# The last quarter of a maxout FFN by Strassen's seven products on row halves of TensorE

## The chip, the core and the metric

The kernel runs on one NeuronCore of one Trainium2 chip. The metric is the device time of one execution in microseconds (us). The kernel before takes 2413.1 us, the median of three runs (2412.13 to 2416.76). The profiled execution spans 2409.3 us from its first to its last instruction.

Engines are written as in the profile: PE is TensorE's matmul, PEld its weight load, DVE VectorE, ACT ScalarE, POOL GpSimd, and SPq, ACTq and POOLq are the queues that issue transfers.

## The reference

All in fp32: a long convolution along the sequence by means of a Fourier transform, and behind it a feed-forward layer that takes the maximum of three products.

```python
# x, v: (4, 12544, 128); pos_emb: (12544, 64)
h_filt = (np.maximum(pos_emb @ w1, 0.0) @ w2) * np.exp(-0.01 * pos)[:, None]
u = x * v
y = irfft(rfft(u, 2 * S) * rfft(h_filt, 2 * S), 2 * S)[:, :S, :]
t = (x * y).reshape(4 * 12544, 128)
# moe_w1..3: (128, 768), moe_w_out: (768, 128)
h = np.maximum(np.maximum(t @ moe_w1, t @ moe_w2), t @ moe_w3)
out = h @ moe_w_out
```

The kernel subtracts `moe_w1` once from the other two, so that each hidden block needs two products (the "up" products): max(a, b, c) = a + max(0, b - a, c - a). The part `a @ w_out` is linear in the token and is one product with a folded matrix, `lin` = moe_w1 @ moe_w_out.

## The kernel before

There are four batches. Each has 32 tiles of 392 tokens (4 x 98), laid out with the 128 model dimensions on the partitions. While the FFN of batch b runs, the convolution of batch b + 1 runs beside it in slots between its products. Beside the last batch nothing runs.

A matmul is always given as two halves of 64 output columns each, which go to the two column halves of the array:

```python
def halves_mm(out, lhsT, rhs, start, stop):
    for h in range(2):
        nc.tensor.matmul(out[64 * h:64 * h + 64], lhsT[:, 64 * h:64 * h + 64], rhs,
                         start=start, stop=stop, skip_group_check=True)      # L132
```

A tile goes through four helpers. `t_load` fetches the tile's part of the convolution's last stage (`zt`) and of x (`xT`). `t_last` makes the token tile `gt`. `up` makes one of six hidden blocks of 128 x 392. `down` adds that block's product with `w_out` to one bank of PSUM and stores the tile after the sixth.

```python
def t_last(i):
    ...
    for s in range(4):
        for a in range(2):
            halves_mm(y[:, s, a * h:a * h + h], zt[:, a, s * D:(s + 1) * D],
                      f4p[:, a, :], s == 0 and a == 0, True)                  # yps
    ... # gt = yps * xT, on DVE (L535)

def up(i, f):
    rhs = gs[i][:].rearrange("d p n -> d (p n)")
    h = hp.tile([P, N], FP32, tag="hid", name="hid")
    pa = hps.tile([P, 512], FP32, tag="hps", name="pa")
    halves_mm(pa[:, 0:N], w_sb[1][:, f * P:(f + 1) * P], rhs, True, True)
    nc.scalar.activation(h[:], pa[:, 0:N], Relu)                              # L545
    pb = hps.tile([P, 512], FP32, tag="hps", name="pb")
    halves_mm(pb[:, 0:N], w_sb[2][:, f * P:(f + 1) * P], rhs, True, True)
    nc.vector.tensor_tensor(out=h[:], in0=h[:], in1=pb[:, 0:N], op=ALU.max)   # L548
    return h

def down(i, f, h):
    if f == 0:
        pos_[i] = ops.tile([D, 512], FP32, tag="ops", name="ops")
        halves_mm(pos_[i][:, 0:N], lin[:], gs[i][:]..., True, False)
    halves_mm(pos_[i][:, 0:N], wo_sb[:, f, :], h[:], False, f == NF - 1)
    if f < NF - 1:
        return
    ...
    nc.scalar.copy(o[:]..., pos_.pop(i)[:, 0:N])                              # L561
    nc.scalar.dma_start(dst, o[:])

for n, (b, i) in enumerate(tiles):          # 4 batches x 32 tiles
    ...
    for f in range(NF):                     # 6 hidden blocks
        ...
        h = up((b, i), f)
        if late is not None:
            down(*late)                     # the block before
        late = ((b, i), f, h)
        if f == 3 and n + 1 < len(tiles):
            t_last(tiles[n + 1])
        ...
```

In the prologue, the filter's little network (`pm`, products on row halves of the array) starts with one group, then a transpose and a product for the window (`window_back`), then the other groups:

```python
warm_up(30)
...
for i in range(9):
    if i < 8:
        mlp_in(i)
    if i == 0:
        window_back()
    if i:
        mlp_out(i - 1)
```

Of the kernel before, what the change touches and what calls it, by code (L numbers as in the profile page):

```python
# [9 lines left out]
FP32 = mybir.dt.float32  # L10
I32 = mybir.dt.int32
U16 = mybir.dt.uint16
ALU = mybir.AluOpType
ACTF = mybir.ActivationFunctionType
PSUM = bass.MemoryType.PSUM
P = 128
# [8 lines left out]
N1 = 90  # L25
# [45 lines left out]
def kernel(  # L71
# [15 lines left out]
    nc = tc.nc  # L87
    NG, _, _, B, NB = x.shape
    FO, S = posT.shape
    D = w2.shape[1]  # L90
# [21 lines left out]
    back_d = nc.inline_tensor(np.eye(P, dtype=np.float32)[:, order].copy(), name="back_const").ap()  # L112
    eye_d = nc.inline_tensor(np.eye(P, dtype=np.float32), name="eye_const").ap()

    w_sb = [const.tile([D, DFF], FP32, name=f"w_sb{i}") for i in range(3)]
    wo_sb = const.tile([P, NF, D], FP32, name="wo_sb")
    lin = const.tile([D, D], FP32, name="lin")
    eye = const.tile([P, P], FP32, name="eye")
    f1 = const.tile([NB, 2 * N1], FP32, name="f1")
    f4 = const.tile([N1, 2, NB], FP32, name="f4")  # L120
    spec = const.tile([P, N1, 2, D], FP32, name="spec")
# [102 lines left out]
    utp = ctx.enter_context(tc.tile_pool(name="utp", bufs=2))  # L224
    pro = ExitStack()
    pin = pro.enter_context(tc.tile_pool(name="pin", bufs=1))
    lwp = pro.enter_context(tc.tile_pool(name="lwp", bufs=3))
    fin = ExitStack()
    inp0 = fin.enter_context(tc.tile_pool(name="inp0", bufs=3))
# [46 lines left out]
    def warm_up(n):  # L276

        ps = fps.tile([P, 1024], FP32, tag="cv", name="pw", bufs=2)
        for _ in range(n):
            halves_mm(ps[:, 0:256], warm[:, 0:P], warm[:], True, True)  # L280

    def window_back():
        pw = fps.tile([P, 1024], FP32, tag="cv", name="pw", bufs=2)
        nc.tensor.transpose(pw[:, 0:64 + HH], win[:], eye[0:64 + HH, 0:64 + HH])
        nc.scalar.copy(winT[:], pw[:, 0:64 + HH])
        nc.tensor.matmul(pw[0:64 + HH, 512:512 + P], winT[:],
                         back[:].rearrange("p r t -> p (r t)"), start=True, stop=True)
        nc.scalar.copy(winr[:].rearrange("n r t -> n (r t)"), pw[0:64 + HH, 512:512 + P])
# [164 lines left out]
    def conv_steps(b, done):  # L453


        out = []

        def at(slot, late, fn, *args):
            out.append((slot, late, len(out), fn, args))

        per_pair = 170 / (NK + 0.6 * (NU - done))
        for u in range(done, NU):
            s = (u - done) * 0.6 * per_pair + 9
            at(max(0, int(s) - 10), 0, u_load, b, u)
            at(int(s) - 6, 0, u_mul, u)
            at(int(s) - 5, 0, u_planes, u)
            at(int(s) - 4, 0, u_dma, u)
            at(int(s), 0, u_join, u)  # L470
            for h in range(2):
                at(int(s + 1 + 0.3 * per_pair * h), 1, u_first, u, h)
        s0 = int((NU - done) * 0.6 * per_pair) + 10
        for g in range(NK):
            s = s0 + int(g * per_pair)
            at(s - 5, 0, w_load, g, 0)
            at(s - 3, 0, h_load, g)
            at(s, 1, g_second, g)
            at(s + 1, 0, w_load, g, 1)
            at(s + 1, 0, g_butterfly, g)  # L480
            at(s + 2, 0, g_swap, g)
            at(s + 3, 0, g_re, g)
            at(s + 4, 0, g_im, g, True)
            at(s + 6, 0, g_unfold, g)
            at(s + 7, 1, g_third, b, g)
        slots = {}
        for s, _, _, fn, args in sorted(out, key=lambda r: r[:3]):
            slots.setdefault(s, []).append((fn, args))
        return slots
# [23 lines left out]
    def t_last(i):  # L513
        zt = zts.pop(i)
        ps = cps.tile([P, 512], FP32, tag="cv", name="yps")
        g = hp.tile([D, 4, NB], FP32, tag="g", name="gt", bufs=2)
        y = ps[:, 0:N].rearrange("d (p n) -> d p n", p=4)
        if i[0] == 0:
            for s in range(4):
                for c in range(2):  # L520
                    halves_mm(y[:, s, :], zt[:, c, s * D:(s + 1) * D], f4[:, c, :],
                              s == 0 and c == 0, c == 1)
        else:

            h = NB // 2
# [3 lines that stand above are left out]
                              f4p[:, a, :], s == 0 and a == 0, True)  # L529
            y = y.rearrange("d p (a m) -> d p m a", a=2)  # L530
        xT = xTs.pop(i)
        if i[0] == 0:
            nc.vector.tensor_tensor(out=g[:], in0=y, in1=xT[:], op=ALU.mult)  # L533
        else:
            nc.vector.tensor_tensor(out=g[:].rearrange("d p (m a) -> d p m a", a=2), in0=y,  # L535
                                    in1=xT[:].rearrange("d p (m a) -> d p m a", a=2),
                                    op=ALU.mult)
        gs[i] = g

    def up(i, f):  # L540
        rhs = gs[i][:].rearrange("d p n -> d (p n)")
        h = hp.tile([P, N], FP32, tag="hid", name="hid")
        pa = hps.tile([P, 512], FP32, tag="hps", name="pa")
        halves_mm(pa[:, 0:N], w_sb[1][:, f * P:(f + 1) * P], rhs, True, True)
        nc.scalar.activation(h[:], pa[:, 0:N], Relu)  # L545
        pb = hps.tile([P, 512], FP32, tag="hps", name="pb")
        halves_mm(pb[:, 0:N], w_sb[2][:, f * P:(f + 1) * P], rhs, True, True)
        nc.vector.tensor_tensor(out=h[:], in0=h[:], in1=pb[:, 0:N], op=ALU.max)  # L548
        return h
# [4 lines that stand above are left out]
            halves_mm(pos_[i][:, 0:N], lin[:], gs[i][:].rearrange("d p n -> d (p n)"), True,  # L554
                      False)
# [3 lines that stand above are left out]
        gs.pop(i)  # L559
        o = op_.tile([D, 4, NB], FP32, tag="o", name="ot")  # L560
        nc.scalar.copy(o[:].rearrange("d p n -> d (p n)"), pos_.pop(i)[:, 0:N])  # L561
        dst = outT.rearrange("d (p b n) -> d p b n", b=B, n=NB)[:, 4 * i[1]:4 * i[1] + 4, i[0], :]
        nc.scalar.dma_start(dst, o[:])

    def run(steps):
        for fn, args in steps:
# [31 lines left out]
        ps = fps.tile([P, 1024], FP32, tag="cv", name="ps1")  # L598
        first_halves(ps, lhs, table, dst, nc.scalar.copy)

    warm_up(30)
    raws.append(load_raw(*jobs[0], nc.sync))
    u_load(0, 0)
    u_load(0, 1)
# [3 lines left out]
    for i in range(9):  # L608
        if i < 8:
            mlp_in(i)  # L610
        if i == 0:
            window_back()
        if i:
            mlp_out(i - 1)
    signs()
# [132 lines left out]


    hp = ctx.enter_context(tc.tile_pool(name="hp", bufs=3))  # L750
    f4p = hp.tile([N1, 2, NB // 2], FP32, name="f4p", bufs=1)
    nc.scalar.dma_start(f4p[:], f4p_d)
    inq = ctx.enter_context(tc.tile_pool(name="inq", bufs=2))
    planes = [hp.tile([P, 2, 4, P], U16, name=f"planes{i}", bufs=1) for i in range(3)]
    for t in planes:
        nc.gpsimd.memset(t[:].rearrange("p h s n -> p (h s n)"), 0)
    op_ = ctx.enter_context(tc.tile_pool(name="op", bufs=2))
    wp = ctx.enter_context(tc.tile_pool(name="wp", bufs=3))
    hh = ctx.enter_context(tc.tile_pool(name="hh", bufs=3))
    cvp = ctx.enter_context(tc.tile_pool(name="cvp", bufs=3))  # L760
    cps = ctx.enter_context(tc.tile_pool(name="cps", bufs=4, space=PSUM))
    hps = ctx.enter_context(tc.tile_pool(name="hps", bufs=3, space=PSUM))
    ops = ctx.enter_context(tc.tile_pool(name="ops", bufs=1, space=PSUM))
    state = {"turn": cps, "pair": (wp, hh), "cv": (cvp, cps), "xb": 3}


    tiles = [(b, i) for b in range(B) for i in range(NT)]
    late = None
    for n, (b, i) in enumerate(tiles):
        if i == 0:  # L770
            beside = {}
            if b + 1 < B:
                beside = conv_steps(b + 1, EARLY if b == 0 else 0)
        if n == 0:
            t_load(*tiles[0])
            t_load(*tiles[1])
            t_last(tiles[0])
        for f in range(NF):

            if i < NT - 2:  # L780
                if f == 0:
                    t_load(*tiles[n + 2])
            elif i == NT - 1 and f < 2 and n + 1 + f < len(tiles):
                t_load(*tiles[n + 1 + f])
            h = up((b, i), f)
            if late is not None:
                down(*late)
            late = ((b, i), f, h)
            if f == 3 and n + 1 < len(tiles):
                t_last(tiles[n + 1])  # L790
            s = i * NF + f
            run(beside.pop(s, ()))
            if s == NT * NF - 1:
                assert not beside, sorted(beside)
    down(*late)


# [35 lines left out]
```

## Time and profile before

| engine | busy us | share of 2409.3 us |
|---|---|---|
| PE | 2393.4 | 99% |
| PEld | 1463.2 | 61% |
| DVE | 1286.4 | 53% |
| ACT | 1026.7 | 43% |
| POOL | 314.2 | 13% |

The chain of waits that ended last is 97% PE. The granted clock of TensorE is 1.0 throughout.

Three habits help with this profile. A program's matmul appears as two records and two weight loads, since fp32 takes two passes; a `halves_mm` is thus four records. A record's duration holds its way through the array too, so the rate is read from the distance of starts. And a row of groups gives busy us, mean ns of one, then the idle time of that engine ahead of the group and what ended it; for an engine that is not the bound, such idle time costs nothing.

### The profile page before, as it was taken

The page shows a single profiled execution, that of the slowest core. Times are in us where ns is not written, and L with a number is a line of the kernel's source. Part 1 is how long each engine was busy: PE and PEld are TensorE (multiplying, and loading weights), DVE is VectorE, ACT ScalarE, POOL GpSimd, SP SyncE. Part 2 cuts the span into 40 slices and gives each one's busy share as a digit, 9 for nine tenths or more (in the row PEclk, how much of TensorE's full clock was granted, in tenths as well). Part 3 has the DMA queues.
Part 4 walks back from the last instruction along what each step waited for, and adds up shares of the span by engine and source line. Part 5 has one row for each costly group of instructions (what it writes and reads, how often), then busy time and mean ns, then how long its engine had stood idle before and what let it go on. Part 6 is the DMA issues. An engine that isn't in the chain of part 4 may idle for free.

```text
span 2409.3 us, 63290 instructions
## 1 busy us (share of the span) xinstructions
PE 2393.4 (99%) x26089; PEld 1463.2 (61%) x26089; DVE 1286.4 (53%) x2719; ACT 1026.7 (43%) x1981; POOL 314.2 (13%) x349
## 2 busy tenths in 40 slices
PE   9999999999999999999999999999999999999999
PEld 8988866655555556666656546666665654444444
DVE  5588834466666645446666644446666642222222
ACT  2688834444444434444444424444444432222222
POOL 2022211011111101101111111101111100000000
PEclk9999999999999999999999999999999999999999
DMA  7778879767767659967777859968777742222221
GB/s 171 179 240 266 278 167 179 162 190 196 214 194 211 175 125 187 182 174 207 219 207 215 219 124 182 189 162 213 214 215 209 215 113 61 55 62 53 64 53 36
DMA packets 544553, 408.21 MB, mean 169 GB/s; under 512 B 390244, under 2 KB 436381, under 8 KB 544265
## 3 DMA queue, kind: packets, MB, share of 16 engines
q1 hardware_dynamic: 421760, 315.25, 53.8%
q10 hardware_dynamic: 117129, 74.31, 10.7%
q0 software_dynamic: 5376, 14.62, 2.1%
q8 instruction: 205, 3.36, 0.6%
q14 instruction: 83, 0.68, 0.1%
HBM read 295.76 MB, written 84.67 MB: 158 GB/s over the span
## 4 chain that ended last, share of the span: by engine, by line
PE 97%; DMA 1%; ACT 1%; DVE 0%; issue 0%; SPq 0%; ACTq 0%; POOL 0%; DVEq 0%
PE ops L132 24%; PE pb L132 21%; PE pa L132 21%; PE ps L132 13%; PE ps L141 7%; PE yps L132 5%; PE sps L688 3%; PE pm L303 1%; PE gps L674 1%; PE pst L341 1%; PE pw L132 1%; DMA hd<-ht 1%; ACT ht L693 0%; DMA xT<-in_x_dram 0%; DVE xt L424 0%
## 5 line engine op out<-in xcount | busy, mean ns | idle before, releaser
L548 DVE TENSOR_TENSOR hid<-hid,pb 128x392 f32<-128x392 f32 x768 | 431.8, 562 | 789.4 <-PE pb L132 510.2
L545 ACT ACTIVATE hid<-pa 128x392 f32<-128x392 f32 x768 | 381.9, 498 | 799.3 <-PE pa L132 630.1
L132 PE MATMUL pa<-gt,w_sb 128*64 128x392 f32 x3072 | 640.7, 493 | 1.1 <-DVE gt L533 1.1
L132 PE MATMUL pb<-gt,w_sb 128*64 128x392 f32 x3072 | 639.6, 492 | 1.4 <-ACT hid L545 1.2
L132 PE MATMUL ops<-hid,wo_sb 128*64 128x392 f32 x3072 | 639.5, 492 | 0.1
L132 PEld LDWEIGHTS pb<-gt,w_sb 128*64 128x64 f32 x3072 | 225.8, 137 | 283.0 <-issue 257.1
L132 PEld LDWEIGHTS ops<-hid,wo_sb 128*64 128x64 f32 x3072 | 227.1, 137 | 278.9 <-issue 228.8
L424 POOL TENSOR_TENSOR xt<-xt,xs 128x512 f32<-128x512 f32 x135 | 172.5, 1278 | 969.6 <-DVE xs L423 778.7
L132 PEld LDWEIGHTS pa<-gt,w_sb 128*64 128x64 f32 x3072 | 201.8, 137 | 111.3 <-issue 67.4
L141 PEld LDWEIGHTS ps<-f,uT 98*64 98x64 f32 x4096 | 178.0, 137 | 47.4 <-issue 44.7
L132 PEld LDWEIGHTS ps<-ab,wt 128*64 128x64 f32 x2880 | 168.4, 137 | 52.4 <-issue 26.8
L132 PE MATMUL ps<-ab,wt 128*64 128x128 f32 x2880 | 190.9, 274 | 1.8 <-DVE ab L431 1.7
L132 PEld LDWEIGHTS ps<-spec,wt 128*64 128x64 f32 x2880 | 168.0, 137 | 37.8 <-issue 34.2
L132 PE MATMUL ps<-spec,wt 128*64 128x128 f32 x2880 | 189.5, 273 | 1.4 <-issue 1.4
L141 PE MATMUL ps<-f,uT 98*64 98x90 f32 x4096 | 188.0, 241 | 0.0
L449 DVE TENSOR_TENSOR zs<-ps,z 128x256 f32<-128x256 f32 x270 | 102.0, 419 | 96.6 <-ACT z L447 94.3
L413 ACT ACTIVATE xs<-xt 64x512 f32<-64x512 f32 x180 | 113.1, 628 | 71.1 <-DVE xt L158 58.9
L431 DVE TENSOR_TENSOR ab<-xt 128x256 f32<-128x256 f32 x360 | 136.0, 419 | 1.6
L419 DVE TENSOR_TENSOR xt<-xt,ht 128x512 f32<-128x512 f32 x180 | 124.2, 690 | 15.6 <-ACT ht L693 15.2
L356 POOL COPY planes<-ut 128x784 uint16<-128x784 uint16 x90 | 76.2, 847 | 426.5 <-DVE ut L336 301.1
L145 ACT COPY spec<-ps 128x360 f32<-128x360 f32 (+1 forms) x132 | 71.8, 546 | 137.0 <-PE ps L141 136.8
L132 PEld LDWEIGHTS yps<-f4p,zt 90*64 90x64 f32 x3072 | 107.3, 138 | 34.4 <-issue 32.3
(86 smaller groups left out, 1824.4 us busy)
## 6 DMA issues: line engine op xcount, KB each, us to landing
wt<-wt_const SPq DMA_DIRECT2D x360, 256.0 KB, 4.8
ht<-hd SPq DMA_DIRECT2D x270, 256.0 KB, 4.5
zd<-zs ACTq DMA_DIRECT2D x180, 256.0 KB, 4.6
zt<-zd SPq DMA_DIRECT2D x192, 180.0 KB, 3.8
ut<-in_xr_dram SPq DMA_DIRECT2D x128, 196.0 KB, 3.6
ut<-in_vr_dram SPq DMA_DIRECT2D x128, 196.0 KB, 4.3
xT<-in_x_dram SPq DMA_DIRECT2D x512, 49.0 KB, 3.0
out_dram<-ot ACTq DMA_DIRECT2D x128, 196.0 KB, 4.0
```

Of the source, the lines that this page charges most:

```text
L132: nc.tensor.matmul(out[64 * h:64 * h + 64], lhsT[:, 64 * h:64 * h + 64], rhs, start=start, stop=stop, skip_group_check=True)
L141: nc.tensor.matmul(ps[64 * c:64 * c + 64, 256 * i + r * N1:256 * i + (r + 1) * N1], a[:, r, :], table[:, c * N1:(c + 1) * N1], start=(i % ...
L145: copy(dst, ps[:].rearrange("p (s m) -> p s m", m=256)[:, :, 0:2 * N1].rearrange("p s (r k) -> p k r s", r=2))
L356: nc.gpsimd.tensor_copy(pl_[:, :, :, 0:NB], a[:].bitcast(U16).rearrange("p s (n h) -> p h s n", h=2))
L413: nc.scalar.mul(xs[0:64], xt[64:128], -1.0)
L419: nc.vector.tensor_tensor(out=xt[:], in0=xt[:], in1=hts[g][:, 0], op=ALU.mult)
L424: (nc.gpsimd if apart else nc.vector).tensor_tensor(out=xt[:], in0=xt[:], in1=xs[:], op=ALU.add)
L431: nc.vector.tensor_tensor(out=ab[:, :, q, :], in0=y[:, :, 0, :], in1=y[:, :, 1, :], op=op)
L449: nc.vector.tensor_tensor(out=zs[:, a], in0=ps[:, 0:256], in1=z1[:], op=op)
L545: nc.scalar.activation(h[:], pa[:, 0:N], Relu)
L548: nc.vector.tensor_tensor(out=h[:], in0=h[:], in1=pb[:, 0:N], op=ALU.max)
L688: nc.tensor.matmul(ps[64 * h:64 * h + 64, (2 * c + k) * 2 * D:(2 * c + k + 1) * 2 * D], G[:, k, c], w2x[:].rearrange("p s d -> p (s d)"), ...
```

## The change

The last batch is handled by pairs of tiles from here on, and two kinds of product are done by Strassen's method (in Winograd's form): a product of 2 x 2 blocks with seven products of blocks and not eight, for extra sums.

- Products with `w_out`: the blocks are tile 1 or 2 of the pair, lower or upper three hidden blocks, lower or upper 64 output columns. A product of blocks has 128 rows of the array, 64 columns, and the 392 tokens are cut into two halves of 196 that go to the two column halves.
- Up products: the blocks are tile 1 or 2, lower or upper 64 model dimensions, lower or upper three hidden blocks. A product of blocks has only 64 rows, so two different ones are issued together, one on the lower, one on the upper rows of the array, into different banks of PSUM. This is done for both up weights, for all pairs but the first, whose hidden blocks are made as before.
- Sums of weights (`tw`, `T`) are made once on DVE and ACT. Sums of tokens (`a_sums`) and of hidden blocks (`s1` to `s4`) are made per pair, mostly on GpSimd. Sums of products are made on DVE out of PSUM.
- The buffers of the convolution are given up before the last batch; `spec`, which held the spectrum, gives space for hidden blocks.
- In the prologue, `window_back` is called within the warm-up.

The purpose is fewer microseconds of TensorE in the stage in which the other engines have room. The core of the diff (cuts marked with ...):

```diff
-    warm_up(30)
+    warm_up(22)
+    window_back()
+    warm_up(3)
...
-        if i == 0:
-            window_back()
...
+    def products(b, i, h, X, Y):
...
+        def mm(ps, w, rhs, start):
+            for c in range(2):
+                nc.tensor.matmul(ps[64 * c:64 * c + 64, 0:H2], w, rhs[:, H2 * c:H2 * c + H2],
+                                 start=start, stop=True, skip_group_check=True)
...
+        plan = (
+            (X, "h11", wo_sb[:, 0:NC, 0:64], True, None, [(copied, "p1", X)], None),
+            (Y, "s2", tw[:, 0], True, None, [(added, "u2", "p1", Y)], None),
+            (X, "h12", wo_sb[:, NC:, 0:64], False, (m1, first), [(copied, "c11", X)], None),
+            (Y, "s3", tw[:, 1], False, (m2, second_), [(added, "u3", "p1", Y)], None),
+            (X, "s1", wo_sb[:, 0:NC, 64:128], True, None, [(added, "c22", "u3", X)], None),
+            (Y, "h22", tw[:, 2], True, (linx[:], second_), [(added, "c21", "u3", Y)],
+             (stored, 0)),
+            (X, "s4", wo_sb[:, NC:, 64:128], False, (m2, first), [(added, "c12", "u2", X)],
+             (stored, 1)),
+        )
...
-    for n, (b, i) in enumerate(tiles):
+    for n, (b, i) in enumerate(tiles[:LAST]):
...
+    conv.close()
...
+    def cycle(i, j, h):            # one of three column blocks of a pair of tiles
...
+        def mm(ps, w, at, rhs, rows, start=False):
+            for c in range(2):
+                nc.tensor.matmul(ps[64 * c:64 * c + 64, 0:N],
+                                 w[rows, at + 64 * c:at + 64 * c + 64], rhs[rows],
+                                 start=start, stop=True, skip_group_check=True)
+        def P1(v): mm(Ys[v], w_sb[1 + v], j * P, g1, LO, True)
+        def P2(v): mm(X_, w_sb[1 + v], j * P, g1, HI, True)
+        def P3(v): mm(Zs[v], w_sb[1 + v], HF_ + j * P, r1, HI)
+        def P4(v): mm(Ys[v], T[v][:, 0], j * P, g2, HI)
+        def P5(v): mm(Zs[v], T[v][:, 0], j * P, r1, LO, True)
+        def P6(v): mm(Ys[v], T[v][:, 1], j * P, r2, HI if v else LO)
+        def P7(v): mm(Ys[v], T[v][:, 2], j * P, r3, LO)
...
+        def hidden(name, a, ps, b=None, at=None):
+            at = at or ps
+            tt(out=at[:, 0:N], in0=new[b], in1=ps[:, 0:N], op=ALU.add)
+            h[name, j] = spare(name)
+            nc.vector.scalar_tensor_tensor(
+                out=h[name, j], in0=new[a], scalar=0.0, in1=at[:, 0:N], op0=ALU.max, op1=ALU.max)
...
+        return {                   # step: [products, what reads them]
+            0: [lambda: P1(a), lambda: copied("p0", Ys[a])],
+            1: [lambda: (P1(b), P2(a)),
+                lambda: (copied("p1", Ys[b]), added("t11", "p0", X_))],
+            2: [lambda: P6(a), lambda: copied("u0", Ys[a])],
+            3: [lambda: P6(b), lambda: copied("u1", Ys[b])],
+            4: [lambda: (P7(a), P2(b)),
+                lambda: (copied("v0", Ys[a]), hidden("h11", "t11", X_, "p1"))],
+            5: [lambda: P7(b), lambda: copied("v1", Ys[b])],
+            6: [lambda: (P5(a), P4(a)), lambda: (h21a(), added("t22", "v0", Zs[a]))],
+            7: [lambda: P4(b), lambda: (h21b(), sums(h, j, 0))],
+            9: [lambda: P3(a), lambda: added("t12", "u0", Zs[a])],
+            10: [lambda: P5(b), lambda: (rest22(), sums(h, j, 1))],
+            12: [lambda: P3(b), lambda: (hidden("h12", "t12", Zs[b], "u1"), sums(h, j, 2))],
+        }
...
+    for i in range(2, NT, 2):
+        h = {}
+        X, Y = banks if i % 4 == 0 else banks[::-1]
+        for j in range(NC):
+            now = cycle(i, j, h)
+            for q in range(7):
...
+                both = [now[q]] + ([before_[q + 7]] if q + 7 in before_ else [])
+                for m in range(2):
+                    for e_ in both[::-1] if m and q in (2, 5) else both:
+                        e_[m]()
+                if (j, q) == (0, 4):
+                    queue += queue_next
+                    queue_next = products(b, i, h, X, Y)
+                some_of(2 if q == 0 or (j, q) == (1, 6) else 1)
...              # loads and t_last of the next pair, its sums of tokens
+            before_ = now
```

Steps 7 to 12 of a column block are issued together with steps 0 to 5 of the next (`before_[q + 7]`), so that each step has one product on the lower and one on the upper rows. `some_of(1)` issues the next product with `w_out` of the pair before; a pair has 25 of these for its 21 steps (21 block products and 4 linear terms).

## The prediction

> **What bounds the kernel now.** I read three things in turn: the page's engine shares, the chain of waits (97% PE), and then only the stage that the change rewrites, the last of the four batches.
>
> ```profile
> PE 2393.4 (99%) x26089; PEld 1463.2 (61%) x26089; DVE 1286.4 (53%) x2719; ACT 1026.7 (43%) x1981; POOL 314.2 (13%) x349
> ```
>
> TensorE is never idle, so only fewer TensorE microseconds can help. The copies of finished output tiles date the stage (timeline of ScalarE):
>
> ```profile
> 1977.32 0.49 ACT L561 COPY ot<-ops 128x392 f32<-128x392 f32 x1 [0.82 <-PE ops L132]
> ...
> 2405.55 0.49 ACT L561 COPY ot<-ops 128x392 f32<-128x392 f32 x1 [1.77 <-PE ops L132]
> ```
>
> The first belongs to the last tile of batch 2, the second to tile 31 of batch 3: 32 tiles in 428.2 us, 13.38 each. The stage by engine (its row of the windows view; columns are the stretch, its length, then busy us and count of PE, PEld, DVE, ACT, POOL):
>
> ```profile
> 1977.00:2410.00 433.00, 428.43 (x3418) 202.88 (x3414) 125.48 (x223) 111.00 (x224) 0.00 (x0) 1.00 0.21 55
> ```
>
> DVE is busy 29% of it, ACT 26%, GpSimd not at all: there is room for additions. The groups in 2000:2300 by shape give the unit costs:
>
> ```profile
> L132 PE MATMUL pa<-gt,w_sb 128*64 128x392 f32 x538 | 111.8, 493 | 0.0
> L132 PE MATMUL ops<-hid,wo_sb 128*64 128x392 f32 x538 | 111.5, 492 | 0.0
> L548 DVE TENSOR_TENSOR hid<-hid,pb 128x392 f32<-128x392 f32 x135 | 76.1, 563 | 191.8 <-PE pb L132 157.6 <-ACT hid L545 34.1
> L545 ACT ACTIVATE hid<-pa 128x392 f32<-128x392 f32 x134 | 66.6, 497 | 204.4 <-PE pa L132 204.4
> L132 PE MATMUL yps<-f4p,zt 90*64 90x49 f32 x704 | 24.0, 221 | 0.0
> ```
>
> A program's matmul is two records (two passes). The two halves of a product run side by side on two column halves of the array, so a product of 392 columns is four records whose starts are two and two, 0.329 us apart: **0.657 us**. One of 196 columns takes half, **0.328**. A tile is 6 x 3 products, one with `lin`, and one `yps` group of 0.93: 18 x 0.657 + 0.657 + 0.93 = 13.4, as measured.
>
> **What the Trainium skill says.** "TensorEngine Tiling (Array Packing)", Tiling Modes: tiles work independently, but "Changing tiling mode (not just tile) drains the TensorE"; 128 rows x 64 columns and 64x64 are listed as different modes. The trace agrees where it can be asked. In the prologue, transposes on the whole array stand between products on column halves:
>
> ```profile
> 66.43 2.63 PE ps L141 x64
> 70.07 2.63 PE ps L141 x64
> ```
>
> These two lines of the chain open one period of 3.64 us. It holds 32 pairs of records at 77.5 ns and 8 transposes at 109 ns (starts of single records in the timeline), 3.35 us; two changes of mode take the other 0.29, **0.145 each**. But every change in this trace that can be measured also changes the column split; none changes rows alone.
> "TensorE: Matmul & The Clock Gate", Part 3 (packing small matmuls), says row and column tiles compose (a packing of 16 tiles measured 10.6x). In this trace row halves occur only in `pm`, with two of the four quadrants in use, so four at once are unproven here. "SBUF — State Buffer", Terms, holds that VectorE and GpSimd share a port pair that is locked for an instruction's length; the one GpSimd sum in this kernel (128x512, 1278 ns) says nothing against it.
>
> **The change part by part.** Times are per pair of tiles, before 2 x 13.38 = 26.8.
>
> 1. Up products. Before: 2 tiles x 6 x 2 = 24 of 0.657 = 15.77. After: seven products for each of two weights and three column blocks, 42, each on 64 rows, one on the lower and one on the upper rows side by side: 21 pairs of 0.657 = 13.80. **-1.97**, in 15 pairs of tiles (the first keeps plain products).
> 2. Products with w_out. Before: 12 of 0.657 = 7.88. After: 7 x 3 of 0.328 = 6.89. **-0.99**, in all 16. The four linear terms (4 x 0.328) equal the two `lin` products before (2 x 0.657).
> 3. Ends of the pipeline: eight of the 630 row products find no partner, so 4 x 0.657 = +2.6.
> 4. Prologue: the window's transpose and product stand between `pm` groups now (20.82 to 21.93 us in the timeline); moved into the warm-up, about **-1.2**.
> 5. Fresh PSUM pools wait for the old ones, and a later store: about +1.5.
>
> Sum on TensorE: -15 x 1.97 - 16 x 0.99 + 2.6 - 1.2 + 1.5 = -42.5, so **2370.6** if nothing waits. A gain over 2% (under 2364.8) is thus out of reach even for a perfect overlap.
>
> 6. Additions. DVE per column block: ten operations of 0.56 = 5.6; per pair of tiles 3 x 5.6, five product sums of about 0.33, two `gt` of 0.57: 19.6 us of some 24, 82%. ACT: 3 x 7 of 0.49 and some copies, 12 us. GpSimd: 12 sums and 4 halves at 1278 x 392/512 = 0.98 us (estimate), 16 us. None is the bound, but DVE is close and in order.
> 7. New waits. A step of the new loop is one row pair and one 196-column product, 0.985 us. From a product's start to its evacuation is 0.87 (pa starts 2000.04, its ACT pass 2000.91), plus 0.50 on ACT and about 0.06 back. So the bank of `h21` (P4, step 6) is free 1.43 after step 6 begins, and P1 of the next block wants it at 0.985: a wait of 0.45 when nothing stands between, 0.12 where an extra product does, none where a `yps` group does. The other weight's P4 runs beside P1 and is read by DVE: free at 0.87 + 0.56 + 0.06 = 1.49, wanted at 1.31: 0.18 each, more when DVE is behind after its three double operations. Together 1.1 to 1.7 us per pair of tiles, **+17 to +25**.
>
> That is 2388 to 2396.
>
> 8. Mode changes. Each of 315 steps goes from row halves to whole rows and back: 630 changes. At 0.145 each: **+91**. The longer step (1.27 us) then covers the waits of 7, so this branch ends at 2370.6 + 91 = 2462.
>
> **The rivals.**
> A, rows alone change without a drain: TensorE shrinks, small waits stay, 2388 to 2396. For it: 90-row and 128-row products follow each other here with no gap, and column tiles run as streams of their own.
> B, each change drains: about 2462, slower. For it: the skill's sentence, and the 27 changes of mode that can be measured, none cheaper than 0.09 us before the first weight load. Half the price (0.07) would give some 2413 plus the small waits.
> C, DVE becomes the bound: 82% by count, so it would have to be held up by GpSimd by a fifth more; worth +20 on top of A, to 2415.
> D, four quadrants don't run side by side: the row pairs take twice their time, 315 x 0.657 = +207, near 2590. Nothing in the trace speaks for it except that it isn't shown.
>
> **Range and chances.** A and B each stand near one half; I lean to A by little, as the pieces that drain here all re-split the columns and these don't. C shifts A upward. I put the time at 2396, on the upper edge of A, and the range from 2374 (waits of 7 nearly absent) to 2468 (B in full). Faster by over 2% needs under 2364.8, below my wait-free sum: 0.03. Slower by over 2% needs above 2461.4: half of B's weight and D, 0.27. The rest, 0.70, is within 2%.
>
> **What the profile would show.** Steps 1 and 2: in the last stage, row products' starts four at a time, 0.329 apart, and some 23 to 24 us from one pair of output stores to the next; under B some 29. The slices of PE stay at 9 under A; under B the timeline has some 0.1 us between the last start plus its stream and the next weight load at every change between `ups` and `ops`. Step 7: PE and PEld waiting for ACT and DVE by `ups`, some 20 us in sum. Step 6: DVE at 7 to 8 tenths in the last seven slices, GpSimd at 6. D would show as row pairs 1.31 us long. Wrong altogether would be a prediction whose DVE operations on PSUM in and out take much longer than 0.56, or whose last stage waits for the loads of `zt` and `xT`, which are hidden now.

## The result, and the profile after

The changed kernel takes **2501.3 us** (median of four runs, 2500.57 to 2501.85); the kernel before takes 2412.6 us beside it. The ratio is **1.036**, with an interval of 1.0345 to 1.0381: slower by 3.6%. The prediction said 2396 and at most 2468. The profiled execution spans 2500.1 us, 90.8 us more than before.

The page of the changed kernel looks as healthy as the one before. Its engine shares, the PE row of its slices, its clock row and its chain of waits by engine:

```profile
PE 2459.0 (98%) x27853; PEld 1448.6 (58%) x27853; DVE 1471.9 (59%) x3082; ACT 1098.9 (44%) x2150; POOL 568.4 (23%) x601
...
PE   9999999999999999999999999999999999999999
...
PEclk9999999999999999999999999999999999999999
...
PE 95%; DMA 2%; issue 1%; ACT 1%; DVE 1%; POOL 0%; SPq 0%; ACTq 0%; DVEq 0%
```

PE has more records than before (27853 against 26089) and is busy 65.6 us longer. No other engine is near its limit. So a reader of the page alone would conclude that TensorE simply got more work. It did not: the busy time of the last stage contains time in which nothing streams.

The date of the stage comes again from the copies of finished tiles (timeline of ScalarE). The last tile of batch 2:

```profile
1983.09 0.48 ACT L564 COPY ot<-ops 128x392 f32<-128x392 f32 x1 [2.41 <-PE ops L131]
```

Before, this row stood at 1977.32. So **5.8 us** were already lost ahead of the rewritten stage in this execution, and the stage, from that row to the end of the span, grew from 432.0 to 517.0 us: **+85.0**.

Two stretches of the stage (windows view; columns as in the prediction: stretch, length, busy us and count of PE, PEld, DVE, ACT, POOL, then granted clock, DMA share and GB/s):

```profile
2130.00:2250.00 120.00, 115.84 (x1260) 44.73 (x1256) 73.42 (x140) 44.27 (x94) 59.30 (x60) 1.00 0.22 52
2250.00:2370.00 120.00, 115.62 (x1256) 44.55 (x1252) 72.40 (x139) 43.56 (x93) 59.09 (x59) 1.00 0.22 52
```

DVE is at 61%, ACT at 37%, GpSimd at 49%, the clock is full, and PE shows 4 us of idle time in 120. The unit costs, from the groups by shape of 2010 to 2480 (busy us, mean ns, idle ahead):

```profile
L965 PE MATMUL ups<-spec,T 64*64 64x392 f32 x1076 | 235.1, 515 | 1.0 <-POOL spec L949 1.0
L592 POOL TENSOR_TENSOR spec<-spec 128x392 f32<-128x392 f32 x178 | 179.5, 1019 | 220.0 <-DVE spec L994 170.4 <-DVE spec L1006 49.5
...
L992 DVE TENSOR_TENSOR upx<-p,upx 128x392 f32<-128x392 f32 x45 | 25.7, 571 | 8.3 <-PE upx L965 8.3
...
L994 DVE SCALAR_TENSOR_TENSOR spec<-t,upx 128x392 f32<-128x392 f32 x45 | 25.3, 563 | 4.5
```

The row products have a mean of 515 ns where the products of the same 392 columns had 493 before. That is a first hint. The loss itself is read from the starts of successive rows in the timeline of PE:

```profile
2202.49 1.14 PE L131 MATMUL yps<-f4p,zt 90*64 90x49 f32 x32 [0.88 <-PE ops L611]
...
2204.38 0.55 PE L611 MATMUL ops<-spec,wo_sb 128*64 128x196 f32 x4
2204.86 0.55 PE L965 MATMUL ups<-spec,T 64*64 64x392 f32 x2
2204.88 0.55 PE L965 MATMUL upz<-spec,w_sb 64*64 64x392 f32 x2
2205.24 0.49 PE L965 MATMUL ups<-spec,T 64*64 64x392 f32 x2
2205.26 0.50 PE L965 MATMUL upz<-spec,w_sb 64*64 64x392 f32 x2
2205.68 0.55 PE L611 MATMUL ops<-spec,wo_sb 128*64 128x196 f32 x4
...
2206.98 0.55 PE L611 MATMUL ops<-spec,wo_sb 128*64 128x196 f32 x4
```

From one `ops` to the next is one step of the new loop: 2205.68 - 2204.38 = **1.30 us**, and again 1.30 to 2206.98. A row pair (0.657) and a product of 196 columns (0.328) make 0.985. So 0.315 us per step is lost, and there is no bracket in these rows: the record of a matmul ends behind its stream, and the next record begins before that end, so PE counts as busy. `ups` and `upz` start 0.02 us apart, so the four quadrants do work side by side. The first row shows another loss, with a bracket: `yps` had to wait 0.88 us.

The queue of weight loads shows what stands between the products (timeline of PEld, same step):

```profile
2204.38 0.20 PEld L611 LDWEIGHTS ops<-spec,wo_sb 128*64 128x64 f32 x4 [0.61 <-issue]
2204.86 0.14 PEld L965 LDWEIGHTS ups<-spec,T 64*64 64x64 f32 x2 [0.28 <-issue]
...
2205.68 0.20 PEld L611 LDWEIGHTS ops<-spec,wo_sb 128*64 128x64 f32 x4 [0.61 <-issue]
```

A weight load normally runs beside the stream of the product before it. Here the load for `ops` starts at 2205.68, where the matmul of `ops` starts too, 0.09 us after the row pair's second pass has streamed out (start 2205.26, 392 columns 0.33, so 2205.59). The load is not early at all: the engine has run dry first.

### The profile page after: what moved, and what is told of

Same layout as the page of the kernel before. It is cut to its first block, busy times and chain, and to the rows that moved or that the text cites. A ratio compares the mean times of both kernels' runs of the same rounds, so it can differ in the third digit from the quotient of the medians.

```text
span 2500.1 us, 68017 instructions
## 1 busy us (share of the span) xinstructions
PE 2459.0 (98%) x27853; PEld 1448.6 (58%) x27853; DVE 1471.9 (59%) x3082; ACT 1098.9 (44%) x2150; POOL 568.4 (23%) x601
## 4 chain that ended last, share of the span: by engine, by line
PE 95%; DMA 2%; issue 1%; ACT 1%; DVE 1%; POOL 0%; SPq 0%; ACTq 0%; DVEq 0%
PE pab L131 30%; PE ops L131 17%; PE ps L131 12%; PE ups L965 9%; PE ps L140 7%; PE ops L611 7%; PE yps L131 5%; PE sps L784 3%; PE upz L965 2%; PE pm L304 1%; DMA hd<-ht 1%; PE pst L342 1%; PE gps L770 1%; PE pw L131 1%; ACT spec L1003 0%
## 5 line engine op out<-in xcount | busy, mean ns | idle before, releaser
L131 PE MATMUL pab<-gt,w_sb 128*64 128x392 f32 x4608 | 863.7, 494 | 2.1 <-ACT hid L549 1.2
L551 DVE TENSOR_TENSOR hid<-hid,pab 128x392 f32<-128x392 f32 x576 | 323.7, 562 | 516.8 <-PE pab L131 285.5
L549 ACT ACTIVATE hid<-pab 128x392 f32<-128x392 f32 x576 | 286.2, 497 | 511.3 <-PE pab L131 429.2
L131 PE MATMUL ops<-hid,wo_sb 128*64 128x392 f32 x2304 | 479.8, 492 | 0.0
L131 PEld LDWEIGHTS pab<-gt,w_sb 128*64 128x64 f32 x4608 | 318.1, 137 | 265.8 <-issue 221.0
L131 PEld LDWEIGHTS ops<-hid,wo_sb 128*64 128x64 f32 x2304 | 170.3, 137 | 208.7 <-issue 168.4
L592 POOL TENSOR_TENSOR spec<-spec 128x392 f32<-128x392 f32 x192 | 195.2, 1028 | 260.7 <-DVE spec L994 172.9
L965 PE MATMUL ups<-spec,T 64*64 64x392 f32 x1080 | 236.0, 515 | 1.0 <-POOL spec L949 1.0
```

What stands on the lines that cost most here:

```text
L592: nc.gpsimd.tensor_tensor(out=h[name, j], in0=h[a, j], in1=h[b, j], op=op)
L965: nc.tensor.matmul(ps[64 * c:64 * c + 64, 0:N], w[rows, at + 64 * c:at + 64 * c + 64], rhs[rows], start=start, stop=True, skip_group_check ...
```

## The experiments

Each was timed in several rounds beside the kernel before on the same chip; a ratio is to that kernel.

The last copy of batch 2 moves between executions even where all code ahead of it is the same. In the profiles of the three kernels with the old front it stands at 1976.86, 1977.32 and 1980.38 us, in four with the front of the changed kernel at 1979.65, 1979.93, 1982.50 and 1983.09. So the change of the stage alone, from that copy to the end of the span, is given beside the times below.

### One change of rows alone, priced in the kernel before

To separate the change of mode from everything else that is new, the kernel before gets 192 products more, one after each hidden block of its last batch. The extra product is small (64 output columns, 49 tokens), its output is read by nobody, and it has either 128 rows (no change of mode) or 64 (a change to row halves and one back; the column split is the same).

```diff
+            if b == B - 1:
+                tick = cps.tile([P, 512], FP32, tag="cv", name="tick")
+                nc.tensor.matmul(tick[0:64, 0:49], w_sb[1][0:64, 0:64],        # tick_full: 0:128
+                                 gs[b, i][0:64, 0:1, 0:49]..., start=True, ...)  # tick_full: 0:128
```

Expected of 128 rows: 

> As the tick on row halves, but the small product uses all 128 rows (64 columns, 49 tokens): no change of mode. Both theories: 192 x some 0.12 us = +23, near 2436; it is the base for the tick on row halves.

Expected of 64 rows: 

> The kernel before, with one small product (64 rows, 64 columns, 49 tokens, result unused) after each product with w_out of the last batch, 192 in all; it uses half of the rows, so TensorE goes into row halves and back at each. If a change of rows alone drains: the small product's own time plus 2 x 0.15 = 0.3 us each, 58 us more than the same with all rows. If only a change of the column split drains: as with all rows.

Measured: with 128 rows **2436.3 us** (ratio 1.0093, 1.0078 to 1.0108), with 64 rows **2489.2 us** (1.0316, 1.0299 to 1.0333). The smaller product costs 52.9 us more (stage alone: 52.4). Divided by 192 this is 0.276 us, or **0.138 us per change of mode**. With 128 rows the small product runs beside its neighbour on the other column half, so the difference need not be the changes alone. The starts of single records with 64 rows give the price in another way: from the end of the stream ahead (2200.386 + 0.329) to the start of `pa` (2201.051) are 0.336 us, of which the two passes of 49 columns take 0.082, and the second pass of `pa` comes 0.051 us late. That is 0.305, or 0.15 per change. Timeline of PEld with 64 rows:

```profile
2200.81 0.19 PEld L793 LDWEIGHTS tick<-gt,w_sb 64*64 64x64 f32 x2 [0.61 <-issue]
2201.05 0.20 PEld L132 LDWEIGHTS pa<-gt,w_sb 128*64 128x64 f32 x4
2201.43 0.14 PEld L132 LDWEIGHTS pb<-gt,w_sb 128*64 128x64 f32 x2 [0.19 <-issue]
2201.76 0.14 PEld L132 LDWEIGHTS pb<-gt,w_sb 128*64 128x64 f32 x2 [0.18 <-issue]
```

Ahead of an ordinary load the queue is idle for 0.18 to 0.19 us, since it is early; ahead of the load for 64 rows it is idle for 0.61, the same signature as in the changed kernel. So it is the change to row halves and back, and not Strassen's sums, banks or helpers, that lets the engine run dry.

### Fewer changes in the changed kernel

If the changes are the loss, the same products in fewer groups must win it back. Instead of one product with `w_out` after every step, several are issued after steps 0, 3 and 6 of a column block, or after steps 0 and 6 only:

```diff
-                some_of(2 if q == 0 or (j, q) == (1, 6) else 1)
+                some_of({0: 3, 3: 3 if j == 0 else 2, 6: 3}.get(q, 0))     # three_groups
+                some_of({0: 5 if j == 0 else 4, 6: 4}.get(q, 0))           # two_groups
```

In `two_groups` the two `t_last` also stand after the groups, at (0, 6) and (1, 0).

Expected of three groups: 

> The changed kernel with the same products, but those with w_out issued in three groups per column block (after steps 0, 3 and 6) and not one after each step. Theory of the mode changes (each entry into or out of row halves costs some 0.157 us: a step is 1.30 us and not 0.985): 24 changes fewer per pair of tiles, 15 pairs, -57, some +5 of waits: 2450. Rival, products on row halves are slow of themselves, or DVE is the bound: no change or slower, 2501 or more.

Expected of two groups: 

> As the three groups, but two per column block (after steps 6 and 0), and both yps groups put where the columns are whole anyway. Theory of the mode changes: 30 changes fewer per pair, -71, the bank's wait gone, -13, row steps that follow each other wait some 0.25 us per block for their copies, +11: 2428. Rival (row products slow, or DVE the bound): within 15 us of 2501.

Measured: three groups **2444.0 us** (1.0130, 1.0115 to 1.0145), two groups **2435.1 us** (1.0088, 1.0071 to 1.0105). Counted from the trace, the stage has 632 changes between row halves and whole rows in the changed kernel, 276 with three groups and 186 with two.

Three groups: 57.3 us less for 356 changes (stage alone: 53.9). Part of that is not theirs: the distance from the last start of `ops` to the first of `yps` shrank from 1.21 to 0.55 us in 13 pairs, which is 8.6. The remaining 45.3 to 48.7 us are **0.127 to 0.137 per change**, close to the price of the small products; it is rather low than high, since new waits for ScalarE's copies came with the grouping.

Two groups went further than three by only 8.9 us (stage alone: 12.9) where 22 were expected, and missed the expected 2428 by 7. The long runs of row products now need their banks of PSUM back faster than ScalarE empties them. Waits of the weight loads, two groups, 2010 to 2480 (us in total, times, longest):

```profile
PEld ups L965 <- ACT u L983: 38.4, 74, 0.7
...
PEld ups L965 <- ACT p L983: 26.3, 44, 0.6
```

Neither row is there in the changed kernel. A part of these 65 us lies beside streams; what they cost can be bounded against the next experiment, which is also free of the `yps` wait: 444 changes fewer should bring 61 to 70 us at 0.138 to 0.158, and 49.9 came (stage alone: 52.9), so some 8 to 20 us went elsewhere, most likely into these waits; no run separates them. The interleaving was there for a reason, and the reason is in conflict with the mode.

### The wait ahead of yps

In the changed kernel `yps` and `q22` (a temporary for the sums of `h22`, one of the four hidden blocks of a column block) share one bank, from a pool that has only that one. `q22` is written and read by DVE in the very step before the first `yps` of a pair; in the row shown above, where `yps` starts at 2202.49, DVE's second pass over it ran from 2201.83 to 2202.39. The edit moves that `t_last` one step later:

```diff
-                    if (j, q) == (0, 3):
+                    if (j, q) == (0, 4):
                         t_last((b, i + 2))
```

Expected: 

> The changed kernel with the token product of the next pair's first tile (yps) issued one step later (step 4, not 3), nothing else. Theory of the bank: yps and the temporary sum of h22 share the one bank of their pool, so yps waits some 0.9 us for two DVE operations in 14 pairs; the move takes that wait away: 2501 - 13 = 2488. Rival, the wait is for the transfer of zt or for TensorE's own order: no change, 2501.

Measured: **2485.0 us** (1.0301, 1.0286 to 1.0317), 16.3 less (stage alone: 13.9). The groups of weight loads for `yps` from 2010 to 2480, first of the changed kernel, then with the later `t_last`:

```profile
L131 PEld LDWEIGHTS yps<-f4p,zt 90*64 90x64 f32 x896 | 30.0, 138 | 16.9 <-PE ops L611 15.7 <-PE ups L965 0.6
```

```profile
L131 PEld LDWEIGHTS yps<-f4p,zt 90*64 90x64 f32 x870 | 30.1, 138 | 1.2
```

The idle time ahead of the group fell from 16.9 to 1.2 us. The profile had put it down to PE (`ops`), whose own work was long done; the wait for several semaphores really ended with DVE's pass over `q22`. In each of the 13 pairs the distance from the last start of `ops` to the first of `yps` fell from 1.21 to 0.16 us, the length of the stream of `ops` itself, so the wait costs 13 x 1.05 = 13.7. The move gives the transfer of `zt` a step more as well, but this rival is out by the trace: the `zt` of the `yps` at 2202.49 had landed at 2179.1.

### Strassen where the mode does not change

Products with `w_out` by seven products have 128 rows like everything around them. This kernel keeps the pairs of tiles and that half of the change, and makes all hidden blocks with plain up products. The sums `T` and `a_sums`, `cycle` and the row halves are left out, and the buffers in `spec` are shared out anew; all of the reference is still computed.

```diff
-        for j in range(NC):
-            now = cycle(i, j, h)
-            ...
+        for q, (name, f) in enumerate(plain):
+            h[name, f] = up((b, i + int(name[1]) - 1), f + (NC if name[2] == "2" else 0),
+                            (b4[2 * q % 4], b4[(2 * q + 1) % 4]), spare(name))
+            if q % 4:
+                sums(h, f, q % 4 - 1)
+            some_of(3 if q == 11 else 2)
+            ...
```

Expected: 

> The last batch by pairs of tiles with seven products for w_out alone; the up products as before, on all rows, so no change of mode. Theory of the mode changes: 16 x 0.99 less than before on TensorE, the later start of the batch (some 6 us by the trace) kept, a longer end: 2413 - 16 + 6 + 2 = 2405. Rival, the seven products and their sums themselves make the loss (DVE, GpSimd, spectrum space as buffers): 2440 or more.

Measured: **2401.6 us** (0.9953, 0.9937 to 0.9969), faster than the kernel before by half a per cent. From the last copy of batch 2 to the last matmul the stage went from 428 to 414 us; 16 x 0.99 = 15.8 was predicted for this half alone. The up products by seven, then, are what turns the gain into a loss, and this kernel still carries the lateness of the front.

### The lateness ahead of the stage

The last batch isn't the only place that the change touches. Windows of the changed kernel near the two ends of the front, and the rows of PE that go with them:

```profile
20.00:22.00 2.00, 2.00 (x44) 2.00 (x42) 0.00 (x0) 0.00 (x0) 0.00 (x0) 0.50 1.10 261
...
321.00:326.40 5.40, 5.30 (x18) 1.97 (x20) 0.61 (x2) 0.99 (x2) 0.00 (x0) 0.50 0.76 164
```

```profile
18.65 20.07 PE L304 MATMUL pm<-w_sb,specH 64*41 64x64 f32 x512 [2.69 <-issue]
...
318.81 1.58 PE L131 MATMUL yps<-f,zt 90*64 90x98 f32 x32 [1.55 <-DMA zt<-zd]
321.10 5.50 PE L131 MATMUL pab<-gt,w_sb 128*64 128x392 f32 x16 [0.71 <-DVE gt L537]
```

With the window's products moved into the warm-up, the warm-up ends at 15.96 us, TensorE is idle for 2.69 us until the data for `pm` are there, and the granted clock falls to one half just when `pm` runs. At 318 us the first `zt` waits for its buffer: `w_sb0` and `eye` had moved into the space that `zt` takes, and folding them into `lin` ends only at 314 us (the chain: `pt`, then DMA `zt<-zd` from 314.01 to 318.67). The idle time there brings half the clock for 5 us more.

Two kernels try to put this right. The first is the changed kernel with a longer warm-up behind the window:

```diff
-    warm_up(3)
+    warm_up(9)
```

Expected: 

> The changed kernel with nine warm-up products behind the window in place of three, all else equal. If the idle time before pm's data costs the clock: no 0.50 in 20 to 22 us, first pm group done about 1.5 us sooner (the ps group that ends at 40.3 at about 38.8), and 2499 to 2500 in all. If the clock falls for another reason: 0.50 stays and the time is 2501.

Measured: **2502.8 us** (1.0368, 1.0349 to 1.0387), not to be told from the changed kernel. The local part is as expected, in the windows and the row of PE:

```profile
20.00:22.00 2.00, 2.00 (x61) 2.00 (x60) 0.62 (x2) 0.00 (x0) 0.00 (x0) 1.00 1.17 251
...
321.00:326.40 5.40, 5.40 (x22) 2.00 (x20) 1.12 (x2) 0.99 (x2) 0.00 (x0) 0.56 1.04 246
```

```profile
18.51 19.04 PE L304 MATMUL pm<-w_sb,specH 64*41 64x64 f32 x512 [0.66 <-issue]
```

The clock is full at 20 us, `pm` takes 19.04 and not 20.07, and the first `ps` group starts at 39.13 and not 40.31. But around 321 us the clock is still one half. The first output copy comes 1.4 us sooner than in the changed kernel (338.15 and not 339.54), which says little, since with an untouched front it came at 336.49 in the run with the later `t_last`. At the end nothing can be measured, where four runs spread over 9 us.

The second takes the Strassen products for `w_out` alone and keeps `w_sb0` and `eye` from start to end, beside the longer warm-up:

```diff
-    w_sb = [None] + [const.tile([D, DFF], FP32, name=f"w_sb{i}") for i in (1, 2)]
+    w_sb = [const.tile([D, DFF], FP32, name=f"w_sb{i}") for i in range(3)]
+    eye = const.tile([P, P], FP32, name="eye")
...
-    warm_up(3)
+    warm_up(9)
```

(To make room, the token tiles of the convolved batches have two buffers and not three, and one `t_last` moves behind the start of the last batch.)

Expected: 

> The seven products for w_out alone, as in the run down_only, and the front of the kernel put right: the first up weight and eye are kept from the start again (zt need not wait for fold), and nine warm-up products and not three stand behind the window, so that TensorE isn't idle before pm's data. Theory (mode changes are the loss in the last batch; the 5.8 us by which the changed kernel was already late before the last batch come from those two places in the front): about 2396, 6 less than down_only's 2402, with the granted clock at 1.0 in 20 to 24 us and around 320 us, and the first tile's output copy near 335 us as before (the changed kernel: 339.5). Rival (the lateness comes from elsewhere, for instance from giving up buffers): 2401 to 2402, first output copy still near 339.

Measured: **2398.5 us** (0.9935, 0.9922 to 0.9947), the fastest version here. The place at 321 us is put right:

```profile
321.00:326.40 5.40, 4.15 (x30) 1.80 (x27) 1.69 (x3) 0.99 (x2) 0.00 (x0) 1.00 0.37 86
```

What this place costs can be read in all profiles: from the last transpose of the fold (`pt`) to the first product with `lin` pass 11.8 to 14.6 us in the six kernels with `w_sb0` in the space of `zt`, and 9.3 to 9.9 us in the four without. So it costs some 2 to 5 us at that point. The place ahead of `pm` isn't the change's alone: in the two kernels with small products, whose front is the old one, TensorE was idle for 2.76 and 4.21 us ahead of `pm`, and its first 64 records took 3.68 and 3.93 us and not 2.74.

But the first output copy came at 337.92 us, not at the 335 expected (before: 334.69; changed kernel: 339.54; without the front's edits: 337.85). In this run 2.00 us went into an idle stretch of PE at 61 to 63 us, to which the profile gives no releaser but "issue", and the first `ps` group ran in 5.59 us, at half clock for part of it, where it took 3.94 before. So the gain over the run without the front's edits, 3 us, agrees with the theory in size but isn't separated from nothing: the two intervals overlap. In the seven profiles with this change the last copy of batch 2 is 2.3 to 5.8 us later than in the kernel before, but in one with the old front it is 3.1 later too; how much the places named cost at the end isn't settled.

## Why the prediction was wrong

**Step 8 failed as a choice, and it is the main cause.** The prediction had both branches and leaned to A, because the changes of mode it could measure all re-split the columns. Rows alone do the same: 0.138 us per change with the small products, 0.127 to 0.137 from three groups, 0.158 from the step of 1.30 us, against the 0.145 that step 8 took from the prologue. "TensorEngine Tiling (Array Packing)", Tiling Modes, the page from the Trainium skill that the prediction quoted, was right in its plain wording, a drain at each change of mode, and the trace agrees. The reservation was not worth half the weight. What should have tipped it is in the same trace: products of 90 and of 128 rows follow each other without a gap, in the changed kernel too (0.16 us from the last start of `ops` to the first of `yps`, as long as the stream between them), and the prediction took this as evidence for A. But 90 rows are more than half of the array too, so neither product runs on row halves, and they say nothing of a change to them.

**Branch B as it was written was too low as well**, 2462 against 2501. Of the 39 us between them, by the profiled execution,

- 8 are the price: the step is 1.30 and not 1.27, 315 times 0.025.
- 14 are the one bank that `yps` and `q22` share. Step 7 looked for waits on the banks of the row products only.
- 6 are the first pair. It keeps its plain products, but the sums of weights run beside it on DVE and ACT, and its up products wait for their evacuations (23.6 us where 24 products of 0.657 and two `yps` groups of 0.93 add up to 17.6). Step 6 counted DVE by pair in the steady state and left the start out. The kernel with Strassen's products for `w_out` alone confirms it: without `T` and `a_sums` the same products take 17.8 us. Some of the waits in the changed kernel (timeline of PE), then in that kernel the first of the 24 products and the first behind them:

```profile
1988.77 1.54 PE L131 MATMUL upz<-gt,w_sb 128*64 128x392 f32 x8 [0.97 <-ACT spec L549]
...
1993.85 0.88 PE L131 MATMUL upz<-gt,w_sb 128*64 128x392 f32 x4 [0.72 <-DVE spec L551]
...
2000.11 1.14 PE L131 MATMUL yps<-f4p,zt 90*64 90x49 f32 x32 [1.47 <-DVE spec L539]
```

```profile
1980.59 1.54 PE L131 MATMUL ups<-gt,w_sb 128*64 128x392 f32 x8 [0.58 <-ACT ot L564]
...
1998.43 1.49 PE L131 MATMUL ups<-spec,w_sb 128*64 128x392 f32 x8
```

- 7 are the front: 5.8 late where step 4 had put it 1.2 early. Some of the 5.8 belongs to this execution: the same front is 2.3, 2.6 and 5.2 late in three others.
- Some 4 are left over. 0.7 of them belong to step 5, below; the others, among them what remains of the waits of step 7, weren't separated.

By the other steps:

**Steps 1 and 2** hold. Row products run side by side in four quadrants; in the long runs of two groups, one row pair follows another at 0.66 to 0.71 us where no bank holds it up. Seven for eight with `w_out` gave about 14 of the 15.8 us.

**Step 3** has nothing against it, but was too small to be seen. **Step 4** had the wrong sign: taking the window's products from between the `pm` groups did save its 1.2 us, as the longer warm-up shows (`pm` takes 19.04 us, and 20.27 with the window in between: 18.15 to 38.42), but the gap they left behind cost the clock, and the fold of `lin` wasn't looked at. **Step 5**: the wait for the old banks is there, 0.58 us, and the end behind the last matmul is 5.6 us long against 4.0, together 2.2 where 1.5 were put.

**Step 6** holds, and **rival C** is out. DVE is at 61% and not 82, because the stage is longer; its operations in and out of PSUM take 0.571 us and GpSimd's sum 1.02 (estimate 0.98). The prediction cited "SBUF — State Buffer", Terms, on a port that VectorE and GpSimd share. Here both work through the stage at 61% and 49%, and the mean of DVE's operations stands where it stood before, at 0.56; no lengthening shows.

**Step 7** in its branch A would have been right in kind: with 1.30 us a step the banks are in time, and the weight loads' waits for L1003 and L1006 lie inside the drain nearly whole. They came back as soon as the drains were taken away, in two groups, and on ScalarE's copies more than at `h21`.

**Rival D** is out by the starts of 0.02 us.

The signs that the prediction named for B were found: the gap of some 0.1 us between the last stream and the next weight load at every change. The pair's length was not 29 us but 31.9: 21 x 1.30, four linear terms of 0.328, two `yps` groups of 0.93 and one wait of about 1 make 31.5.

## What to carry to other kernels

Before small products are interleaved with large ones, write down the tiling mode (rows x columns) of each and count the changes: at about 0.13 to 0.16 us each here, a change costs as much as a quarter of a 392-column product, and the seven-for-eight saving on row halves, 2 us in a pair of tiles, pays for some 13 of them, not for 42. A page whose PE row is full of nines doesn't show it; starts of successive matmuls, and the idle time ahead of a weight load that is no longer early, do. A saving that keeps the mode of its surroundings (here the products with `w_out`, 0.65% together with the repaired front) may be worth taking alone out of a larger change.

## What the runs showed of the hardware

- A change between 128 rows and row halves, columns unchanged, costs 0.127 to 0.137 us (356 changes fewer: 45.3 to 48.7 us), 0.138 us (192 small products there and back: 52.9 us) or 0.158 us (steps of 1.30 us for 0.985 of streams). The next weight load starts about 0.09 us after the last stream's end, and the first part of it is then exposed: first passes of `ups` are 0.38 us ahead of the second, and not 0.33.
- Four 64 x 64 quadrants take four streams at once, their starts within 0.02 us.
- The granted clock fell to 0.50 after idle times that are shorter than expected: after 2.25 to 3.18 us ahead of `pm` in six kernels (2.69 in the changed one), and after 1.55 and 0.71 us with 1.6 us of work between them at 321. The Trainium skill, "TensorE: Matmul & The Clock Gate", Part 1, gives one idle window of about 3.4 us for this. Before the first `ps` group, 1.58 us of idle time cost the clock in four kernels (the changed one: 5.59 us for 96 records), and 1.58 to 1.65 us did not in six (with the longer warm-up: 3.94), so the same gap can go either way.
